# wq's first heads in one wide transfer at both ends of a decode kernel, w4 with two rows in a run, w3's weights with a step of two

## The chip, the cores and the metric

The kernel runs on one core of a Trainium2 chip. The metric is the device time of one execution in microseconds, as the median of several runs; smaller is better. The engines are named as in the profile: PE multiplies matrices (PEld is its loading of weights), DVE works on vectors, ACT computes activations, POOL is the general engine, and SP issues most transfers. Sixteen DMA engines carry the transfers.

## The reference

Two layers of attention with a cache and a small mixer with an MLP, for 8 rows of one token each:

```python
def _A_ref(x, k_cache, v_cache, wq, wo):      # x: 8 x 1 x 448
    q = (x @ wq) -> 16 heads of 256           # 8 K/V heads, each for 2 q heads
    scores = q . k * 256 ** -0.5              # 4096 cached keys
    o = softmax(scores) @ v
    return o @ wo
def _B_ref(x, w1, w2, w3, w4):
    x1 = x + shifted(gelu(norm(x) @ w1)) @ w2 # one token: every shift leaves zeros
    return x1 + gelu(norm(x1) @ w3) @ w4      # w3: 448 x 1792, w4: 1792 x 448
x = x + _A_ref(norm(x), ...); x = x + _B_ref(norm(x), ...)     # twice, same weights and cache
```

With one token the shifted part is zero, so the mixer comes down to the MLP on a norm of a norm. All inputs are bf16. The K and V caches hold 128 MiB each and are read in both layers, but for what stays in SBUF between them.

## The kernel before, in words

**Units and items.** The 8 K/V heads are taken in four pairs, gp 0 to 3. A unit is (ps, b, gp): layer ps (0 or 1), row b, pair gp. A unit has four K tiles and four V tiles of 1 MiB each (128 x 4096 bf16). `block` writes the order of the work out by hand, as a list of items: (unit, 0, c) is K tile c, (unit, 1, c) is V tile c, and (task, 2, 0) is a set of weights. Units of gp 2 and 3 of one row come in layer 0 and right behind it in layer 1, and some of their tiles (`kept`, `inner`, `part`) stay in SBUF or PSUM in between, so that they are read once.

**What an item does.** A K tile is turned by DVE in blocks (L1000), then PE computes scores (L1015), tiles 0 and 1 together and 2 and 3 together; ACT takes the exponential (L1024). A V tile is multiplied with the probabilities (L1083; in the last row's units with V as the weights, two columns apart, L1099). When a row has all its heads, a chain of small steps follows: scaling, wo (L180, L453), norm, w3, gelu, w4, the next layer's q. After each row's units come stages in which only V tiles are left, with the chain's steps between.

**Places and the queue.** SBUF has NC = 17 places of 1 MiB (L61). `emit_loads` (L939) runs after each item: it takes the next load of the list and issues it on SP as soon as a place is free, strictly in order; when the first in line has no place, it stops. A K pair wants two neighbouring places and one transfer of 2 MiB (L918, `load_k`): `reserve` (L881) holds two neighbours for it, free now or free within SOON = 8 items, and the line waits for them. Where none can be held, the two tiles go as single transfers of 1 MiB. V tiles go at L932, or in two halves at L935 in the stages with the chain. Each transfer waits on SP until what read its place before is done.

**Weights.** q of the first eight heads (gp 0 and 1) is computed from wq's first 2048 columns, which don't stay in SBUF. They are loaded again when needed, 1024 columns (one gp) into one place: `weights("q", (gp, r0, r1))` makes an item for gp and rows r0 to r1, `load_weights` (L980) issues three runs of 128 rows in one transfer (L989) and the last 64 rows by `load_tail` (L976), and the item computes q with `tail_cols` and `project_rows` (L391, L371). This is done seven times: gp 0 and gp 1 at the start for all rows of layer 0 (L799), three times under way for layer 1 (`q_rows`, L706), and at the end for gp 1, rows 5 to 7, and gp 0, row 7 (`q_final`, L707, L812 and L816). wq's other half, wo's second half, w3 and w4 stay in SBUF and are loaded at the start (L1143 to L1150); w4 by

```python
    nc.sync.dma_start(w4_sb[:], B_w4.rearrange("(c p) d -> p c d", p=128))
```

so that partition p holds rows p, 128 + p and so on, each a run of 448 elements (896 B). Block c of the hidden layer (128 of 1792) is computed from w3 by `wblk` (L214), which gives 128 neighbouring columns as weights, in `mlp_hidden` (L474) and in the last row's end (L1544); w4 is then read by block c (`w4_of`, and L1588 at the end).

**The end.** After the last V tile come its product, wo, the norm, w3 (L1544), gelu, w4 (L1588) and the transfer of the result (L1599).

Of the kernel before, what the change touches and what calls it, by code (L numbers as in the profile page):

```python
# [17 lines left out]
def kernel(  # L18
# [27 lines left out]
    nc = tc.nc  # L46
    Bn, Sq, D = A_x.shape
# [4 lines left out]
    Hq = HD // Dh  # L52
    F = B_w3.shape[1]
    assert Sq == 1 and Hq == 2 * G and Dh == 256 and S == 4096 and G % 2 == 0
    assert D == 448 and F % 256 == 0
    GP = G // 2
    NB2 = HD // 128
    HC = F // 128
# [163 lines left out]

    def rows_to_cols(row, nb):

# [236 lines left out]
    def mlp_hidden(b0, nb):  # L464

        yield from norm(xT[:, :, b0 : b0 + nb], nb, True)
        h_ps = room_ps("h", nb)
        for c in range(HC):
            for fc in range(4):
                w, xi = wblk(w3_sb, F, c, fc)  # L470
                if nb == 1:
                    wide(h_ps[:, c : c + 1], w, xbs(1)[:, xi, :], fc == 0, fc == 3)
                    continue
                nc.tensor.matmul(  # L474
                    h_ps[:, c * nb : c * nb + nb],
                    w,
                    xbs(nb)[:, xi, :],
                    start=(fc == 0),
                    stop=(fc == 3),
                )  # L480
            if c in (4, 9, HC - 1) if nb == 1 else c % 7 == 6:
                yield 0 if c == HC - 1 else None
        g_t = chn.tile([128, HC * MID], FP32, tag="g")
        hh = g_t[:, 0 : HC * nb]
        g0 = g_t[:, HC : 2 * HC] if nb == 1 else misc[:, 456 : 456 + HC * nb]
        if nb == 1:
            HT_t = chn.tile([128, HC, 1], BF16, tag="HT")
            HT = HT_t[:]
        else:
            HT = HTw[:, :, b0 : b0 + nb]  # L490

        nc.vector.tensor_scalar_mul(hh, h_ps, 0.5)
        nc.vector.scalar_tensor_tensor(g0, hh, 4 * 0.044715, hh, ALU.mult, ALU.mult)
        nc.vector.scalar_tensor_tensor(g0, g0, 1.0, hh, ALU.add, ALU.mult)
        nc.scalar.activation(g0, g0, ACT.Tanh, scale=2 * 0.7978845608028654)
        yield 0
        nc.vector.scalar_tensor_tensor(
            HT,
            g0.rearrange("p (c b) -> p c b", b=nb),
            1.0,  # L500
            hh.rearrange("p (c b) -> p c b", b=nb),
            ALU.add,
            ALU.mult,
        )
        yield 2
        return HT
# [197 lines left out]
    ]  # L704

    q_rows = {4: (0, 0, 4), 5: (1, 0, 5), 7: (0, 4, 7)}  # L706
    q_final = [(1, 5, 8), (0, 7, 8)]  # L707

    o_rows = {0: [(0, 4, 0, 3), (4, 8, 0, 1)], 3: [(0, 4, 3, 8), (4, 8, 3, 5)]}
    o_late = {1: (4, 8, 1, 2), 2: (4, 8, 2, 3), 5: (4, 8, 5, 8)}  # L710
# [42 lines left out]
    def weights(kind, rows):  # L753

        n = len(tasks)
        tasks.append((2, rows, kind))
        items.append((n, 2, 0))
# [37 lines left out]
        items.extend(due[:n])  # L795
        del due[:n]

    for gp in free:
        weights("q", (gp, 0, Bn))  # L799
    before = None  # L800
    for k in begin:
        block(k, before)
# [2 lines left out]
    for b in range(Bn):  # L805
        k3, k2 = ((1, b, gp) for gp in keep[::-1])
        block(k3)
        block(k2, k3)
        if b + 1 < Bn:
            first_kept(b + 1, ahead[b + 1], k2)  # L810
        else:
            weights("q", q_final[0])  # L812
            before = k2
            for k in final_units:
                if k == final_units[2]:
                    weights("q", q_final[1])  # L816
                block(k, before)
                if before == k2:
                    weights("o", None)
                before = k  # L820
            block(None, before)
# [117 lines left out]
    def emit_loads(most=None):  # L939
        n = 0  # L940
        while loads and places and n != most:
            it = loads[0]
            k, kv, c = it
            mate = (k, 0, c + 1)
            if kv == 0 and c % 2 == 0 and paired(k, c) and mate in loads[:4]:
                if it not in held:
                    reserve(it, mate)
                if it in held:
                    p = held[it]
                    if p in places and p + 1 in places:  # L950
                        del held[it], held[mate]
                        taken(it, p)
                        taken(mate, p + 1)
                        load_k(it, p, 2)
                        n += 1
                        continue
                    break
            open_ = open_places()
            if not open_:
                break  # L960
            p = pick(open_)
            taken(it, p)
            n += 1
            if kv == 2:
                load_weights(slots[p], tasks[k][2], tasks[k][1])
            elif kv:
                load_v(it, slots[p])
            else:
                both = c == 1 and (k, 0, 2) in loads[:2] and p + 1 in open_
                if both:  # L970
                    taken((k, 0, 2), p + 1)
                load_k(it, p, 1 + both)
# [7 lines left out]
    def load_weights(dst, kind, rows):  # L980

        if kind == "o":
            nc.sync.dma_start(
                dst[:, 0 : WI * D].rearrange("p (h x) -> p h x", x=2 * D),
                A_wo[0 : WI * 128].rearrange("(h p j) d -> p h (j d)", p=128, j=2),
            )
            return
        src = A_wq[:, HU * rows[0] : HU * rows[0] + HU]
        nc.sync.dma_start(  # L989
            dst[:, 0 : 3 * HU].rearrange("p (f c) -> p f c", f=3),  # L990
            src[0:384].rearrange("(f p) c -> p f c", f=3),
        )
        load_tail(dst[:, 3 * HU : 3 * HU + HU // 2], src)

    def transpose_k(t):

# [121 lines left out]
    nc.scalar.dma_start(x_row, A_x.rearrange("b s d -> (b s) d"))  # L1118
    tails = NC - 4
    places.remove(tails)  # L1120
    emit_loads(2)
    ps0 = rows_to_cols(x_row, Bn)
    nc.vector.tensor_copy(xT[:], ps0)
    emit_loads(5)
# [22 lines left out]
        A_wo[WI * 128 :].rearrange("(h p j) d -> p h (j d)", p=128, j=2),  # L1147
    )
    load_split(w3_sb, B_w3, F)
    nc.sync.dma_start(w4_sb[:], B_w4.rearrange("(c p) d -> p c d", p=128))  # L1150
    run(norm(xT[:], Bn, False))

    gens, pairs_done, p_of = [], {}, {}
# [104 lines left out]
        nc.scalar.copy(ptw[:, ring_of[it], :, 6:8], psv[slot_of[it[0]]][:, it[2]])  # L1258

    rz_gp = None  # L1260
    kept_q = items[12]

    for idx, it in enumerate(items):
        if idx == len(items) - 2:
# [24 lines left out]
        if kv == 2:  # L1289
            rows = b  # L1290
            if gp == "o" and rows is None:
                end_wo = slot
                early_rows(0, HH, 0, MID, 1, slot)
                add_gen("rest", rest(), idx + 1, idx + 18, 20)
            elif gp == "o":
                for who in rows:
                    early_rows(*who, 0, slot)
            else:
                gp_q, r0, r1 = rows
                nb = r1 - r0  # L1300

                def q_of_block(c, fc, qw=slot):
                    if fc < 3:
                        return qw[:, fc * HU + 128 * c : fc * HU + 128 * c + 128], fc
                    k = 2 * 128 * c // HU
                    at = 3 * HU + 128 * c - k * HU // 2
                    return qw[:, at : at + 128], 3 + k

                ps_q = (
                    store[0][:, 256 : 256 + 8 * nb] if nb == Bn else misc[:, 192 : 192 + 8 * nb]  # L1310
                )
                cols = tail_cols(r0, r1, misc[:, 320 : 320 + nb], slot[:, 4 * HU - 128 :])
                project_rows(q_of_block, 4 * gp_q, 4, r0, r1, ps_q, cols)
                if idx > 1:
                    q_rows_done.update((r, gp_q) for r in range(r0, r1))
        elif kv == 0:
            if (ps, b) not in state:
                if ps == 1:
# [133 lines left out]
                pairs_done[ps, b] = pairs_done.get((ps, b), 0) + 1  # L1452
                free_slots.append(slot_of.pop(n))
        if kv == 2:
            if gp == "q" or rows is not None:
                places.append(p)
        elif not (ps == 0 and stays(it)):
            if (ps, gp, kv, c) == (1, keep[1], 1, homes[0]):
                where[(b, part[0]), part[1:]] = p
                moves.extend(part_words(slot))  # L1460
            elif (ps, gp, kv, c) == (1, keep[1], 1, homes[1]):
                where[(b, inner[0]), inner[1:]] = p
                moves.extend(inner_words(slot))
            elif kv == 0 and kept_now:
                if c % 2 == 0:
                    places.extend([p, where[(b, gp), (0, c + 1)]])
            elif not late(it):
                places.append(p)
            elif c % 2:
                places.extend([where[n, 0, c - 1], p])  # L1470
# [69 lines left out]
    for f0, f1 in ((0, 3), (3, 4)):  # L1540
        for c in range(HC):
            for fc in range(f0, f1):
                w, xi = wblk(w3_sb, F, c, fc)
                nc.tensor.matmul(  # L1544
                    h_ps[:, c * nb : c * nb + nb],
                    w,
                    xe[:, xi, :],
                    start=(c + fc == 0),
                    stop=(fc == 3),
                    skip_group_check=True,  # L1550
                )
# [80 lines left out]
```

## Time and profile before

The runs took 1036.71 to 1040.44 us.

| what | value |
|---|---|
| median of 3 runs | 1037.01 us |
| profiled execution | 1035.63 us, its span 1033.6 us |
| PE matmul busy | 655.7 us (63%), 12739 instructions |
| DVE busy | 597.4 us (58%) |
| ACT busy | 211.6 us (20%) |
| HBM read | 419.63 MB, 406 GB/s over the span |
| wq loads of 768 KB and of 128 KB | 7 and 7, 12.9 and 12.4 us from issue to landing |
| w4's load (1568 KB) | 1, 15.1 us from issue to landing |
| K loads of 2048 KB and of 1024 KB | 86 and 20 |
| granted TensorE clock, mean | 0.631 |

The profile is that of one execution. Busy shares are averages over stages with different limits; the slices (40 equal parts of the span, a digit or a rate for each) show how they follow each other. A row of a group gives the line, the engine, the operation, its shapes and count, the busy time and the mean of one in ns, and then the idle time just before and what ended it. A row of the timeline gives the start and the time taken in us and how many instructions were merged; for SP, the time of a merged row spans the waits inside it. A row of a window gives the busy time and count of PE, PEld, DVE, ACT and POOL, the granted clock, the DMA engines' share and GB/s. The trace also holds a record of every DMA packet, with its start, its length and its bytes.

### The profile page before, as it was taken

How to read it: one execution, taken by the hardware profiler on the slowest of the kernel's cores; microseconds unless marked ns; L12 is line 12 of the kernel's file. 1: busy time of each engine (PE TensorE's matmuls, PEld its weight loads, DVE VectorE, ACT ScalarE, POOL GpSimd, SP SyncE). 2: the span in 40 equal slices, each digit the busy share in tenths (PEclk: the TensorE clock that was granted, in tenths of full speed). 3: DMA queues.
4: the chain of work that ended last, by engine and by line, in shares of the span. 5: the costliest groups of instructions: out<-in, count | busy, mean ns of one | idle time of the engine just before them, and what ended most of it. 6: DMA issues, size and time to landing. Idle time of an engine off the chain costs nothing.

```text
span 1033.6 us, 28857 instructions
## 1 busy us (share of the span) xinstructions
PE 655.7 (63%) x12739; PEld 417.7 (40%) x12739; DVE 597.4 (58%) x1407; ACT 211.6 (20%) x685; POOL 16.4 (2%) x27
## 2 busy tenths in 40 slices
PE   3144544875577567755785578557756875586775
PEld 2022222553345334533453346334533553355544
DVE  6334567148825871597249725792597259725572
ACT  0011111131214120412041214121412141214110
POOL 0000000000000000000000000000000000000000
PEclk9976555566666556655566665556665575656655
DMA  9999999999999999999999999999999999999994
GB/s 364 390 426 420 423 423 419 390 424 424 416 402 422 424 417 401 419 425 398 407 412 425 418 399 412 423 418 399 426 424 416 401 414 425 418 401 411 418 422 199
DMA packets 68141, 421.51 MB, mean 408 GB/s; under 512 B 6952, under 2 KB 12848, under 8 KB 43312
## 3 DMA queue, kind: packets, MB, share of 16 engines
q1 hardware_dynamic: 67968, 419.66, 99.1%
q8 instruction: 100, 1.64, 0.6%
q14 instruction: 25, 0.20, 0.0%
q10 hardware_dynamic: 48, 0.01, 0.0%
HBM read 419.63 MB, written 0.01 MB: 406 GB/s over the span
## 4 chain that ended last, share of the span: by engine, by line
DMA 43%; DVE 27%; PE 22%; issue 3%; SPq 3%; ACT 2%; POOL 0%; DVEq 0%; ACTq 0%
DMA places<-in_A_v_cache_dram 28%; DVE places L1000 22%; DMA places<-in_A_k_cache_dram 14%; PE sc L1015 9%; PE o L1083 6%; PE misc L592 2%; PE misc L180 2%; ACT p_n L1024 2%; DVE qbd L415 1%; DVE store L1046 1%; DMA places<-in_A_wq_dram 1%; PE misc L529 1%; SPq L932 1%; SPq L199 1%; PE misc L1066 1%
## 5 line engine op out<-in xcount | busy, mean ns | idle before, releaser
L1000 DVE STREAM_TRANSPOSE places<-places 128x512 uint32<-128x512 uint32 (+1 forms) x576 | 455.1, 853 | 39.8 <-DMA places<-in_A_k_cache_dram 39.3
L1015 PE MATMUL sc<-places,qbd 128*8 128x256 bf16 (+1 forms) x4768 | 236.3, 352 | 164.8 <-DVE places L1000 163.9
L1083 PE MATMUL o<-places,ptw 128*8 128x256 bf16 x3808 | 242.9, 380 | 129.4 <-DMA places<-in_A_v_cache_dram 100.6
L1015 PEld LDWEIGHTS <-qbd 128*8 128x8 bf16 x4768 | 124.2, 105 | 231.6 <-DVE places L1000 123.5
L1083 PEld LDWEIGHTS <-ptw 128*8 128x8 bf16 x3968 | 102.4, 101 | 192.7 <-issue 116.6
L1024 ACT ACTIVATE p_n<-sc 128x256 bf16<-128x256 f32 x128 | 95.5, 746 | 351.0 <-PE sc L1015 346.8
L1258 ACT COPY ptw<-psv 128x32 bf16<-128x32 bf16 x248 | 52.8, 227 | 175.4 <-PE o L1083 173.8
L415 DVE CAST qbd<-misc 32x16 bf16<-32x16 f32 (+1 forms) x184 | 30.8, 168 | 62.0 <-PE misc L409 60.2
L592 PE MATMUL misc<-R_t,o_t 128*128 128x4 f32 (+1 forms) x212 | 45.5, 321 | 29.1 <-DVE qbd L415 12.4
L592 PEld LDWEIGHTS misc<-R_t,o_t 128*128 128x128 f32 x212 | 41.2, 271 | 45.4 <-issue 16.6
L532 DVE RECIPROCAL rz<-misc 128x4 f32<-128x4 f32 (+1 forms) x55 | 9.6, 175 | 83.1 <-PE misc L529 45.7
L1073 ACT CAST psv<-misc 128x128 bf16<-128x128 f32 x64 | 17.0, 266 | 188.1 <-PE misc L1066 188.1
L1051 ACT COPY places<-store 128x1024 bf16<-128x1024 bf16 x40 | 40.2, 1027 | 11.0 <-PE o L1083 11.0
L529 PE MATMUL misc<-zm,one 128*128 128x4 f32 (+1 forms) x110 | 28.0, 326 | 17.0 <-DVE zm L521 13.0
L529 PEld LDWEIGHTS misc<-zm,one 128*128 128x128 f32 x110 | 23.2, 263 | 32.8 <-DVE zm L521 16.0
L180 PEld LDWEIGHTS <-w_sb 128*128 128x128 bf16 x896 | 27.7, 105 | 16.7 <-issue 16.7
L1024 ACT ACTIVATION_READ_ACCUMULATOR p_n<-sc 128x1 f32 x128 | 33.9, 265 | 0.0
L546 ACT COPY o_t<-o 128x256 f32<-128x256 f32 x53 | 19.8, 373 | 47.0 <-PE o L1083 47.0
L295 POOL TENSOR_TENSOR t<-t,nhalf 128x2 f32<-128x2 f32 (+2 forms) x18 | 12.0, 671 | 951.4 <-DVE t L316 951.4
L1046 DVE TENSOR_SCALAR store<-places 128x512 uint32<-128x512 uint32 x40 | 25.0, 678 | 0.0
L1066 PEld LDWEIGHTS <-p_n 128*128 128x128 bf16 x256 | 11.5, 105 | 30.0 <-issue 18.9
L596 DVE CAST qT<-misc 128x8 bf16<-128x8 f32 (+1 forms) x37 | 7.2, 195 | 27.0 <-PE misc L592 20.3
(158 smaller groups left out, 368.8 us busy)
## 6 DMA issues: line engine op xcount, KB each, us to landing
places<-in_A_k_cache_dram SPq DMA_DIRECT2D x86, 2048.0 KB, 14.3
places<-in_A_v_cache_dram SPq DMA_DIRECT2D x194, 512.0 KB, 7.2
places<-in_A_v_cache_dram SPq DMA_DIRECT2D x87, 1024.0 KB, 18.2
places<-in_A_k_cache_dram SPq DMA_DIRECT2D x20, 1024.0 KB, 11.8
places<-in_A_wq_dram SPq DMA_DIRECT2D x7, 768.0 KB, 12.9
rest<-in_A_v_cache_dram SPq DMA_DIRECT2D x8, 640.0 KB, 14.2
places<-in_A_v_cache_dram SPq DMA_DIRECT2D x8, 384.0 KB, 13.1
wo_sb<-in_A_wo_dram SPq DMA_DIRECT2D x1, 2688.0 KB
```

Of the source, the lines that this page charges most:

```text
L180: nc.tensor.matmul(bass.AP(out.tensor, out.offset, [out.ap[0], (1, WIDE)]), w, x.to_broadcast([128, WIDE]), start=start, stop=stop, skip_g ...
L415: nc.vector.tensor_copy(qbd[32 * a : 32 * a + 32, :, g0 : g0 + ng, a, :], qs.rearrange("p e (f g u h) -> p (e f) u g h", f=2, u=2, h=2)[:, ...
L529: nc.tensor.matmul(z_ps, ones, zm[:], start=True, stop=True)
L592: nc.tensor.matmul(ot_ps[:, j], o_sb[:].rearrange("p (i j) -> p j i", j=2)[:, j], R, start=True, stop=True)
L1000: nc.vector.transpose(w, w)
L1015: nc.tensor.matmul(sc[32 * k : 32 * k + 8, 128 * (x % 2) : 128 * (x % 2 + nx)], qbd[:, ep, gp % 2].rearrange("p a h -> p (a h)"), v, start ...
L1024: nc.scalar.activation(p_sb[:, :, :, 2 * u : 2 * u + 2].rearrange("p t i x -> p x t i"), sc[:, 0:256].rearrange("p (x t i) -> p x t i", x= ...
L1046: nc.vector.tensor_single_scalar(kept_words.bitcast(U32), words.bitcast(U32), 0, op=ALU.bitwise_or)
L1051: nc.scalar.copy(words, kept_words.bitcast(BF16))
L1066: nc.tensor.matmul(pt_ps[:, t], p_sb[:, t].rearrange("p i x -> p (i x)"), cols, start=True, stop=True,)
L1083: nc.tensor.matmul(o_ps[32 * q : 32 * q + 8, :], ptz[:, at : at + 8], v[:, y * Dh : (y + 1) * Dh] if v2 is None or y < PR else v2[:, (y - ...
L1258: nc.scalar.copy(ptw[:, ring_of[it], :, 6:8], psv[slot_of[it[0]]][:, it[2]])
```

## The change

Three edits, and what they carry with them:

- At the start and at the end the two wq loads become one of a new kind, "q2": 2048 columns into two neighbouring places, one item, one `tail_cols` for the rows of both, and then both projections. The last row's gp 0 is thereby computed with gp 1's rows, ahead of the final units, and not before the third of them. The list of items is one shorter from the start on, and two at the end.
- `emit_loads` gives a "q2" load the place p only where p + 1 is open too, and else stops.
- w4 is loaded so that two of its rows lie in one run (1792 B) for 12 of 14 blocks, in three transfers; w3's blocks take every second of 256 columns to fit that order (`w3blk`), and two of the 14 blocks stay as they were.

```diff
+    def w3blk(c, fc):
+
+        at = fc * F + 128 * c if fc < 3 else 3 * F + 128 * (c % 7)
+        xi = fc if fc < 3 else 4 - c // 7
+        if c % 7 == 6:
+            return w3_sb[:, at : at + 128], xi
+        at -= 127 * (c % 7 % 2)
+        return w3_sb[:, at : at + 255 : 2], xi
...
-                w, xi = wblk(w3_sb, F, c, fc)
+                w, xi = w3blk(c, fc)
...
-    q_final = [(1, 5, 8), (0, 7, 8)]
+    q_first = ((0, 0, Bn), (1, 0, Bn))
+    q_final = ((1, 5, 8), (0, 7, 8))
...
-    for gp in free:
-        weights("q", (gp, 0, Bn))
+    weights("q2", q_first)
...
-            weights("q", q_final[0])
+            weights("q2", q_final)
             before = k2
             for k in final_units:
-                if k == final_units[2]:
-                    weights("q", q_final[1])
                 block(k, before)
...
+            wide_q = kv == 2 and tasks[k][2] == "q2"
+            if wide_q:
+                open_ = [p for p in open_ if p + 1 in open_]
+                if not open_:
+                    break
             p = pick(open_)
             taken(it, p)
             n += 1
+            if wide_q:
+                places.remove(p + 1)
+                free_at[p + 1] = free_at[p]
...
-        src = A_wq[:, HU * rows[0] : HU * rows[0] + HU]
+        at, n = (0, HF) if kind == "q2" else (HU * rows[0], HU)
+        src = A_wq[:, at : at + n]
         nc.sync.dma_start(
-            dst[:, 0 : 3 * HU].rearrange("p (f c) -> p f c", f=3),
+            dst[:, 0 : 3 * n].rearrange("p (f c) -> p f c", f=3),
             src[0:384].rearrange("(f p) c -> p f c", f=3),
         )
-        load_tail(dst[:, 3 * HU : 3 * HU + HU // 2], src)
+        load_tail(dst[:, 3 * n : 3 * n + n // 2], src)
...
-    emit_loads(2)
+    emit_loads(1)
...
-    nc.sync.dma_start(w4_sb[:], B_w4.rearrange("(c p) d -> p c d", p=128))
+    w4_rows = B_w4.rearrange("(k x) d -> k x d", k=2)
+    w4_to = w4_sb[:].rearrange("p (k c) d -> p k c d", k=2)
+    for k in range(2):
+        nc.sync.dma_start(
+            w4_to[:, k, 0:6].rearrange("p (c j) d -> p c (j d)", j=2),
+            w4_rows[k, 0:768].rearrange("(c p j) d -> p c (j d)", p=128, j=2),
+        )
+    nc.sync.dma_start(w4_to[:, :, 6], w4_rows[:, 768:].rearrange("k p d -> p k d"))
```

The projection loop of the item takes its columns from both places where the kind is "q2" (768 rows of runs of 2048 B become 384 runs of 4096 B; the last 64 rows come in runs of 2048 B where they came in runs of 1024 B).

More of the change, by code (lines that the diff above doesn't have):

```diff
@@ L54 @@
     assert Sq == 1 and Hq == 2 * G and Dh == 256 and S == 4096 and G % 2 == 0
-    assert D == 448 and F % 256 == 0
+    assert D == 448 and F == 14 * 128
     GP = G // 2
@@ L963, in emit_loads @@
             n += 1
+            if wide_q:
+                places.remove(p + 1)
+                free_at[p + 1] = free_at[p]
             if kv == 2:
-                load_weights(slots[p], tasks[k][2], tasks[k][1])
+                load_weights(places_t[:, p * PB : (p + 1 + wide_q) * PB], tasks[k][2], tasks[k][1])
             elif kv:
@@ L1260 @@
     rz_gp = None
-    kept_q = items[12]
+    kept_q = items[11]
     for idx, it in enumerate(items):
@@ L1298, with q_of_block @@
             else:
[L1299 to L1310, printed above, removed]
-                )
[L1312 to L1315, printed above, removed]
+                n_gp = 2 if gp == "q2" else 1
+                parts = rows if n_gp == 2 else [rows]
+                n_w = n_gp * HU
+                qw = places_t[:, p * PB : (p + n_gp) * PB]
+                r_at, r_to = parts[0][1:]
+                cols = tail_cols(
+                    r_at, r_to, misc[:, 320 : 320 + r_to - r_at], qw[:, n_gp * PB - 128 :]
+                )
+                for gp_q, r0, r1 in parts:
+                    nb = r1 - r0
+                    def q_of_block(c, fc, c0=(n_gp - 1) * 8 * gp_q):
+                        at = 128 * (c0 + c)
+                        if fc < 3:
+                            return qw[:, fc * n_w + at : fc * n_w + at + 128], fc
+                        k = 2 * at // n_w
+                        at += 3 * n_w - k * n_w // 2
+                        return qw[:, at : at + 128], 3 + k
+                    ps_q = (
+                        store[gp_q][:, 256 : 256 + 8 * nb]
+                        if nb == Bn
+                        else misc[:, 192 : 192 + 8 * nb]
+                    )
+                    project_rows(
+                        q_of_block,
+                        4 * gp_q,
+                        4,
+                        r0,
+                        r1,
+                        ps_q,
+                        lambda xi: cols(xi)[:, r0 - r_at : r1 - r_at],
+                    )
+                    if idx > 0:
+                        q_rows_done.update((r, gp_q) for r in range(r0, r1))
         elif kv == 0:
@@ L1454 @@
         if kv == 2:
-            if gp == "q" or rows is not None:
-                places.append(p)
+            if rows is not None:
+                places.extend([p, p + 1] if gp == "q2" else [p])
         elif not (ps == 0 and stays(it)):
@@ L1542 @@
             for fc in range(f0, f1):
-                w, xi = wblk(w3_sb, F, c, fc)
+                w, xi = w3blk(c, fc)
                 nc.tensor.matmul(
```

## Prediction

> **What bounds the kernel now.** I read the page's slices first, then the waits by group, then the DMA queue's own list in the stretches that the change touches, then the tail.
>
> ```profile
> span 1033.6 us, 28857 instructions
> ...
> DMA  9999999999999999999999999999999999999994
> GB/s 364 390 426 420 423 423 419 390 424 424 416 402 422 424 417 401 419 425 398 407 412 425 418 399 412 423 418 399 426 424 416 401 414 425 418 401 411 418 422 199
> ...
> L1083 PE MATMUL o<-places,ptw 128*8 128x256 bf16 x3808 | 242.9, 380 | 129.4 <-DMA places<-in_A_v_cache_dram 100.6
> ```
>
> The DMA row is 9 in every slice but the last: the 16 engines move 419.6 MB without a pause. PE's PV matmuls idle 129.4 us, 100.6 of them for V. In the trace's packet records the engines are full from about 7 us to 1022 us. So the time is the start, plus packet time over 16, plus a tail of some 11.6 us after the last V piece (1022.0 to 1033.6). Two things move it: shorter packet time, or a moment in which the engines run dry, which nothing gives back later because they never rest later.
>
> The profiled execution is 1035.63 us (span 1033.6 and 2.0 around it); the median of the runs is 1037.01, 1.4 more. I sum differences and add them to the median.
>
> **Packets (removed work).** Mean time of one packet, from the packet records of the whole trace: 896 B 46.5 ns, 1024 B 46.2, 1792 B 78.2, 2048 B 91.2, 4096 B 165.2, 8192 B 315.3, 16384 B 623.8.
> - w4 lands early (45.1 to 52.4 us); its 1792 packets of 896 B took 46.0 ns there, 1792 B ones (wo, just ahead) 79.1. Now 1792 x 46.0 = 82.4 us; after 768 x 79.1 + 256 x 46.0 = 72.5 us. Over 16 engines: -0.62 us.
> - Each pair of wq loads has 768 packets of 2048 B and 256 of 1024 B (81.9 us); after, 384 of 4096 B and 128 of 2048 B (75.1 us): -0.42 us. Two pairs: -0.84. At the start 2048 B packets took 101.6 ns, elsewhere 85.6 between wq packets alone, so the first pair may give 0.23 to 0.95.
> - Start: the second wq load is late to reach the engines:
>
> ```profile
> 4.50:6.50 2.00, 0.61 (x2) 0.50 (x2) 0.78 (x6) 0.00 (x0) 0.43 (x1) 1.00 0.73 212
> ```
>
> DMA share 0.73 over 2 us is 0.54 us lost. With two issues fewer (about 1.4 us of SP) K stands ready sooner: 0 to -0.54, I take -0.3.
>
> The Trainium skill, "DMA: Bandwidth & Descriptors", Specifications, gives 512 B as the smallest transfer at line rate; by it all these packets would run at one rate. The rows disagree (896 B in 46.5 ns is 19 B/ns, 8192 B in 315.3 is 26), so I keep the rows, and that rule stands below as a rival.
>
> **Two neighbouring places (added wait).** The wide load needs places p and p+1 open, and emit_loads stops when the first in line can't go: what stands behind it on SP waits too. It also shifts which place every later load gets. Both programs as built load in the same order; 306 tiles get another place. For each load, the item after which it can go is set against the trace: when PE ends that item, and when the bytes ahead of the load have landed. The second less the first is the queue's lead. Now it is 1.6 us at the least, with full engines; in the changed program it is less than that in two spots alone.
>
> *Spot 1, K of (pass 1, b 1, gp 0), around 550 us.* Now its tiles 0 and 1 go as two single loads after (1,3,2)'s scores, 2 and 3 as one after a V item:
>
> ```profile
> 526.27 15.38 SPq L918 DMA_DIRECT2D places<-in_A_k_cache_dram  x5
> 541.70 0.43 SPq L932 DMA_DIRECT2D places<-in_A_v_cache_dram  x1
> 550.58 0.33 SPq L918 DMA_DIRECT2D places<-in_A_k_cache_dram  x1
> ```
>
> In the changed program tiles 0 and 1 go together after the V item that ends at 538.7, and tiles 2 and 3 are tied to places 0 and 1, which hold K tiles 0 and 1 of (1,0,0). Those are read by the scores that end at 550.5, and the V load behind waits with them:
>
> ```profile
> 544.40 2.43 DVE L1000 STREAM_TRANSPOSE places<-places 128x1024 uint32<-128x1024 uint32 x3
> 547.05 5.86 DVE L1000 STREAM_TRANSPOSE places<-places 128x1024 uint32<-128x1024 uint32 x7
> 549.51 1.02 PE L1015 MATMUL sc<-places,qbd 128*8 128x256 bf16 x16
> ```
>
> Those scores can't come sooner: DVE turns their K from 544.4 on, behind the q projection and the K ahead of it, at 2.4 us a tile, all data landed. All that was issued before tiles 2 and 3 has landed at 547.0 (bytes summed over the packets). So the engines are dry from 547.0 to the first packets of a load issued at 550.58. How long from issue to packet on idle engines: the wq load issued at 929.95 has its first at 931.52, 1.57 us; the first load of the program 1.1 us, with all 16 engines busy after some 2.0. I take 1.6: 550.58 + 1.6 - 547.0 = **+5.2 us**. Bounds: 4.7 to 5.6 by the two rows, and 0 if the scores came early enough. (The same page, Latency and other measured facts, has 0.6 us to the first byte; by it the sum would be 1.0 us less. The row says 1.57.) The K in question then lands near 557, and DVE needs it near 560, so compute doesn't notice; the next V stage, which waits for V, then runs 5 us late.
>
> *Spot 2, the last wide load, near 930 us.*
>
> ```profile
> 925.12 2.81 SPq L935 DMA_DIRECT2D places<-in_A_v_cache_dram  x3
> 929.95 0.38 SPq L989 DMA_DIRECT2D places<-in_A_wq_dram  x1
> 930.38 0.55 SPq L976 DMA_DIRECT2D places<-in_A_wq_dram  x1
> 931.87 2.34 SPq L918 DMA_DIRECT2D places<-in_A_k_cache_dram  x3
> ```
>
> At 929.95 one place comes free (a V), which serves wq now. A pair comes free only with the kept K's scores, which release the next line at 931.87. So wq goes 1.9 us later, its first packets near 933.4. The V still outstanding at 930.0 is 239 packets of 4096 B: 239 / 16 x 165 ns = 2.5 us, to 932.5 on the mean engine. That is 1.0 us dry, of which 0.2 is there now (14.8 busy engines around 931): **+0.8**, bounds 0 and 1.9. Behind it SP has K at once.
>
> **At nothing.** (a) The second final projection moves some 20 items earlier: 32 weight loads and matmuls at L371 (0.9 us) and a few DVE rows, one tail_cols less; its two DMAs pass K of (1,5,1) and (1,6,1), wo and a V, which land 2.2 us later and have 8 us and more of lead. The end waits for V that was issued 17 us ahead, and hides it; without that cover it costs about 1 us. (b) At the start both projections wait for all of wq, near 7 us, but the norm ends at 8.3 anyway. (c) w3's weights with a step of two elements: 48 of each 56. The trace has such a load already, L1099 (V's every second column), beside the plain ones:
>
> ```profile
> L1099 PEld LDWEIGHTS <-places 128*128 128x128 bf16 x256 | 7.5, 104 | 6.6 <-DMA places<-in_A_v_cache_dram 6.2 <-issue 0.4
> L1544 PEld LDWEIGHTS <-w_sb 128*128 128x128 bf16 x56 | 1.8, 107 | 0.6 <-issue 0.6
> ```
>
> 104 against 107 ns: nothing.
>
> **Sum.** -0.62 - 0.84 - 0.3 + 5.2 + 0.8 = +4.2 us: 1039.9 for the profiled execution, **1041.3** on the median, +0.41%. A measurement of this kernel tells about 0.5% (5.2 us) from no change, so this counts as the same, on the slow side.
>
> **Rivals.**
> - *Not slower: the bytes alone.* If DVE reaches (1,0,0) some 5 us sooner against the queue, spot 1 closes. For it: the lead in items there (9) is more than the smallest now (6). Against: DVE is busy without a gap from 531 to 540 and from 544.4 on. Then -1.76 + 0.8, or -1.76 with spot 2 covered too: 1035.3 to 1036.1. Chance 0.18.
> - *Slower by over 0.5%: spot 1 is longer.* The engines refill late after running dry, as at the start, where the second load takes until 6.5 us to fill all 16 although issued by 2.8. Of that delay, 1 to 2 us more would fall on the same gap; it decides when the gap passes 6.2 us. 1042.3 to 1043.3. Chance 0.14.
> - *Strided weights cost.* If each of the 48 in the final w3 pass stood alone on the path at 105 ns: +5.0 in the tail, 1046.3. Against: L1099. Chance 0.04.
> - *Packets of 896 B and up all run at one rate* (the rule above): the 1.46 us of packets aren't saved: 1042.7. Against: the packet rows. Chance 0.04.
>
> My forecast has 0.60, with its own range of 1040 to 1042.5 (its top passes +5.2 with about 0.05). Faster by over 0.5% would need 5.2 us less, three times all packets saved: 0.01. Slower by over 0.5%: 0.05 + 0.14 + 0.04 + 0.04 = 0.27. Within: 0.72. The range that holds 8 in 10: 1036.0 to 1044.0, which takes in the bytes alone and the longer gap.
>
> **What would show it.** Right: in the changed profile SP issues one 2 MB K load and a V right after scores, near 550, after a pause of some 12 us; the GB/s drops there by about 5 us' worth in one slice, the V waits of the stage after lie 5 us later; packets of 896 B fall from some 1800 to 264 and w4 lands in 0.6 us less; wq's last load comes from L1005 right after scores near 932; L1544's successor keeps 105 ns. Wrong: full DMA through 550 (then the first rival), a w3 pass longer than 1.7 us, or an end that no longer waits for V.

## The result and the profile after

The changed kernel takes 1040.38 us (median of 16 runs, 1037.75 to 1042.96) against 1037.02 us for the kernel before on the same chips (16 runs): a ratio of 1.0029, 95% interval 1.0018 to 1.0040, so 1.9 to 4.1 us slower. Forecast was +4.2 us and 1041.3 us. The profiled execution of the changed kernel took 1042.26 us, 1.9 above its median; where times are compared, the medians and ratios are meant, and the profile is used to see where the time lies.

The page of the changed kernel, its slices first, then the group of the PV matmuls (the lines have moved by some 16; L1083 is now L1099, L1015 is L1031, L1000 is L1016; the L1099 that the prediction shows, V's every second column, is L1115 now):

```profile
span 1040.2 us, 28728 instructions
...
DMA  9999999999999999999998999999999999999994
GB/s 377 394 428 421 420 424 419 401 423 422 416 403 425 426 412 397 419 406 407 390 415 335 420 408 416 425 418 378 425 425 417 403 418 423 417 394 404 422 421 194
...
L1099 PE MATMUL o<-places,ptw 128*8 128x256 bf16 x3808 | 246.0, 383 | 133.9 <-DMA places<-in_A_v_cache_dram 105.4
```

One slice stands out: number 22 (546 to 572 us) has 335 GB/s where it had 425, and its DMA digit is the one 8 among the 9s. PE's wait for V grew from 100.6 to 105.4 us. The next view is SP's own list around that slice in the changed kernel (start, time, engine, line, transfer, count; the first row is a merged one and spans its waits):

```profile
526.23 12.61 SPq L925 DMA_DIRECT2D places<-in_A_k_cache_dram  x3
```

```profile
550.70 0.33 SPq L925 DMA_DIRECT2D places<-in_A_k_cache_dram  x1
551.08 0.42 SPq L939 DMA_DIRECT2D places<-in_A_v_cache_dram  x1
```

After a K load near 538.8 SP issues nothing until 550.70. Before, it issued another K load near 541.3 and a V load at 541.70. What released it at 550.70 are PE's scores, which themselves wait for DVE. The two rows of PE in the changed kernel, with the idle time before and its releaser in brackets, and DVE's:

```profile
548.45 1.03 PE L1031 MATMUL sc<-places,qbd 128*8 128x256 bf16 x16 [4.70 <-DVE places L1016]
...
549.63 1.02 PE L1031 MATMUL sc<-places,qbd 128*8 128x256 bf16 x16
```

```profile
544.52 2.43 DVE L1016 STREAM_TRANSPOSE places<-places 128x1024 uint32<-128x1024 uint32 x3
...
547.16 7.05 DVE L1016 STREAM_TRANSPOSE places<-places 128x1024 uint32<-128x1024 uint32 x9
```

The scores end at 550.65 and the load goes 0.05 us later. The window of 545 to 555 us (columns as before: busy time of PE, PEld, DVE, ACT, POOL, granted clock, DMA share, GB/s), in the kernel before:

```profile
545.00:555.00 10.00, 5.18 (x96) 3.23 (x100) 9.89 (x19) 1.16 (x5) 0.00 (x0) 0.50 1.02 428
```

and in the changed one:

```profile
545.00:555.00 10.00, 5.07 (x96) 3.15 (x100) 9.89 (x19) 1.05 (x4) 0.00 (x0) 0.50 0.53 197
```

PE, PEld and DVE have the same number of instructions in it, and DVE is busy for 9.89 of 10 us in both. The DMA share falls by 0.49 over 10 us, which is 4.9 us of all 16 engines. From the packet records, the mean engine is dry (has no packet in flight) for 4.7 us between 540 and 556. The last load ahead of the gap ends with one small record of 4 B on each engine: these 16 end from 546.35 to 548.75, at 547.05 on the mean. The first new packet starts at 551.67, the sixteenth at 552.27, and the mean of these 16 is 551.86.

The start of the kernel after, 4.5 to 6.5 us, shows the small gain there (DMA share 0.73 before; 0.22 more over 2 us is 0.4 us):

```profile
4.50:6.50 2.00, 0.61 (x2) 0.50 (x2) 0.77 (x5) 0.00 (x0) 0.44 (x1) 1.00 0.95 346
```

### The profile page after: what moved, and what is told of

Same layout as the page of the kernel before. It is cut to its first block, busy times and chain, and to the rows that moved or that the text cites. A ratio compares the mean times of both kernels' runs of the same rounds, so it can differ in the third digit from the quotient of the medians.

```text
span 1040.2 us, 28728 instructions
## 1 busy us (share of the span) xinstructions
PE 663.0 (64%) x12673; PEld 420.1 (40%) x12673; DVE 597.3 (57%) x1403; ACT 211.6 (20%) x685; POOL 16.4 (2%) x27
## 4 chain that ended last, share of the span: by engine, by line
DMA 42%; DVE 28%; PE 22%; ACT 2%; issue 2%; SPq 2%; POOL 0%; DVEq 0%; ACTq 0%
DMA places<-in_A_v_cache_dram 27%; DVE places L1016 23%; DMA places<-in_A_k_cache_dram 14%; PE sc L1031 9%; PE o L1099 6%; PE misc L601 2%; PE misc L180 2%; DVE store L1062 2%; ACT p_n L1040 2%; DVE qbd L424 1%; PE misc L538 1%; DMA places<-in_A_wo_dram 1%; SPq L199 1%; PE misc L1082 1%; PE misc L380 0%
## 5 line engine op out<-in xcount | busy, mean ns | idle before, releaser
L1016 DVE STREAM_TRANSPOSE places<-places 128x512 uint32<-128x512 uint32 (+1 forms) x576 | 455.4, 854 | 46.7 <-DMA places<-in_A_k_cache_dram 46.5
L1031 PE MATMUL sc<-places,qbd 128*8 128x256 bf16 (+1 forms) x4704 | 238.9, 357 | 163.3 <-DVE places L1016 162.1
L1099 PE MATMUL o<-places,ptw 128*8 128x256 bf16 x3808 | 246.0, 383 | 133.9 <-DMA places<-in_A_v_cache_dram 105.4
L1031 PEld LDWEIGHTS <-qbd 128*8 128x8 bf16 x4704 | 123.3, 105 | 232.3 <-DVE places L1016 124.8
L1099 PEld LDWEIGHTS <-ptw 128*8 128x8 bf16 x3968 | 102.8, 101 | 198.1 <-issue 121.6
L601 PE MATMUL misc<-R_t,o_t 128*128 128x4 f32 (+1 forms) x212 | 47.6, 331 | 32.2 <-DVE qbd L424 16.9
L601 PEld LDWEIGHTS misc<-R_t,o_t 128*128 128x128 f32 x212 | 43.3, 284 | 49.4 <-issue 22.0
```

The lines of the kernel that those rows point to most:

```text
L601: nc.tensor.matmul(ot_ps[:, j], o_sb[:].rearrange("p (i j) -> p j i", j=2)[:, j], R, start=True, stop=True)
L1016: nc.vector.transpose(w, w)
L1031: nc.tensor.matmul(sc[32 * k : 32 * k + 8, 128 * (x % 2) : 128 * (x % 2 + nx)], qbd[:, ep, gp % 2].rearrange("p a h -> p (a h)"), v, start ...
L1099: nc.tensor.matmul(o_ps[32 * q : 32 * q + 8, :], ptz[:, at : at + 8], v[:, y * Dh : (y + 1) * Dh] if v2 is None or y < PR else v2[:, (y - ...
```

## The experiments

The theory on record: the wide loads shift the places of all loads behind them; one K pair then has to wait for a pair of places that is read late, the DMA engines run dry, and that time is lost. Its main rival: the wait is hidden by what lies in SBUF, and the time comes from w3's weights with a step of two, or from the moved projection. All kernels below were timed in turn with the kernel before, in two sets: 29 runs of it in each (medians 1037.50 and 1037.61 us), 12 of each variant, and 6 of place8. The dry times come from the one execution of each that was profiled.

**old_places: the places alone, without the change.**

```diff
 # the kernel before, emit_loads
-            p = pick(open_)
+            p = (10, 11)[n] if kv == 2 and now[0] == 0 else pick(open_)
```

> The kernel before with one thing altered: the two first wq loads go to places 10 and 11 in place of 0 and 1. Nothing of the change is in it. The plan of places then ties K tiles 2 and 3 of (1,1,0) to a pair that is read by the scores of (1,0,0), as in the changed kernel. Theory 1 (the time comes from the place wait near 550 us): SP issues that K load some 9 us later than before, the DMA engines are dry for 4.5 to 5 us there, and the time is 4.5 us above the kernel before (ratio 1.0045). Theory 2 (the wait is hidden by what is stored ahead, and the changed kernel's extra time comes from the w3 weights with a step of two or from the projection that was moved): no difference, ratio 1.000.

Measured: 1041.08 us, ratio 1.0033 (1.0018 to 1.0049). Nothing was computed or loaded otherwise than before, and the time of the changed kernel came back. SP's list in this kernel:

```profile
550.62 0.33 SPq L918 DMA_DIRECT2D places<-in_A_k_cache_dram  x1
551.00 0.43 SPq L932 DMA_DIRECT2D places<-in_A_v_cache_dram  x1
```

and its window:

```profile
545.00:555.00 10.00, 5.14 (x96) 3.17 (x100) 9.89 (x19) 1.12 (x5) 0.00 (x0) 0.50 0.51 186
```

The engines are dry for 5.0 us. Theory 2 can't explain this time: there is no w3 step and no moved projection here. The ratio of 1.0045 that was expected lies inside the interval, near its top.

**place10: the whole change, with other places.**

```diff
 # the changed kernel, emit_loads
-            p = pick(open_)
+            p = 10 if wide_q and now[0] == 0 else pick(open_)
```

> The changed kernel, with its first wide wq load put at places 10 and 11 in place of 0 and 1; by the plan no K pair then waits near 550 us. Theory 1: the dry stretch is gone, the time is 4.7 us below the changed kernel and 1.2 to 1.7 us below the kernel before (ratio 0.9985). Theory 2: it stays where the changed kernel is, ratio 1.003.

Measured: 1036.40 us, ratio 0.9992 (0.9980 to 1.0005). Its interval lies below that of the changed kernel. No dry time from 540 to 556:

```profile
545.00:555.00 10.00, 5.13 (x96) 3.17 (x100) 9.89 (x19) 1.11 (x5) 0.00 (x0) 0.50 1.00 423
```

By this kernel's plan tiles 2 and 3 of (1,1,0) get places 3 and 4, which come free with the q item; they go at 542.5 with the V behind them, and the load released by the scores at 550.6 is already the next K pair, (1,2,0):

```profile
524.14 18.73 SPq L925 DMA_DIRECT2D places<-in_A_k_cache_dram  x4
542.97 0.38 SPq L939 DMA_DIRECT2D places<-in_A_v_cache_dram  x1
550.62 0.33 SPq L925 DMA_DIRECT2D places<-in_A_k_cache_dram  x1
```

The gain over the kernel before (0.8 us by the ratio) is less than the 1.2 to 1.7 expected and not told from none.

**place8: a second wait of the kind.** The same line with 8 in place of 10.

> The changed kernel with its first wide wq load at places 8 and 9. By the plan the K pair near 550 us waits as in the changed kernel, and a second one, tiles 2 and 3 of (1,5,0) near 870 us, waits too, with a lead of -2.4 us. Theory 1: two dry stretches, 4.7 and about 4 us, so 4 us above the changed kernel, ratio to before 1.007. Theory 2: as the changed kernel, 1.003.

Measured: 1044.54 us, ratio 1.0067 (1.0044 to 1.0090), 3.9 us above the changed kernel by the ratios. Both stretches of this kernel are dry, the second for 5.2 us (4 expected):

```profile
545.00:555.00 10.00, 5.55 (x104) 3.35 (x104) 9.89 (x19) 1.52 (x5) 0.00 (x0) 0.50 0.51 185
860.00:870.00 10.00, 4.99 (x104) 2.93 (x104) 9.89 (x18) 1.83 (x7) 0.00 (x0) 0.71 0.49 179
```

The second lies where the plan of places said. Twice the wait makes about twice the time, by 6 runs.

**w4_alone: w4 and w3 without the wide loads.**

```diff
 # the kernel before, with the change's w3blk and its three w4 transfers
-                w, xi = wblk(w3_sb, F, c, fc)
+                w, xi = w3blk(c, fc)
...
-    nc.sync.dma_start(w4_sb[:], B_w4.rearrange("(c p) d -> p c d", p=128))
+    for k in range(2):
+        nc.sync.dma_start(
+            w4_to[:, k, 0:6].rearrange("p (c j) d -> p c (j d)", j=2),
+            w4_rows[k, 0:768].rearrange("(c p j) d -> p c (j d)", p=128, j=2),
+        )
+    nc.sync.dma_start(w4_to[:, :, 6], w4_rows[:, 768:].rearrange("k p d -> p k d"))
```

> The kernel before with the w4 and w3 edit alone; places as before. Theory 1: w4 lands with 0.6 to 0.7 us less packet time, the w3 pass at the end is as long as before (1.5 to 1.6 us for 56 weight loads), ratio 0.9993. Theory 2 (the step of two costs): the w3 pass is longer and the time 1 to 5 us above the kernel before, ratio 1.001 to 1.005.

Measured: 1036.79 us, ratio 0.9988 (0.9976 to 1.0000). The two w3 passes with the step (first the one for rows 0 to 3, then the one at the end) have the same mean as with plain weights. The first row below is of the kernel before, where L474 is what is now L483 (the end's plain row, L1544, stands in the prediction); the others are of this kernel:

```profile
L474 PEld LDWEIGHTS <-w_sb 128*128 128x128 bf16 x56 | 1.9, 107 | 0.1
```

```profile
L483 PEld LDWEIGHTS <-w_sb 128*128 128x128 bf16 x56 | 1.8, 107 | 0.0
L1560 PEld LDWEIGHTS <-w_sb 128*128 128x128 bf16 x56 | 1.8, 107 | 0.6 <-issue 0.6
```

So the step of two costs nothing that shows (107 ns in all three rows), and no sign of the 1 to 5 us of theory 2 is left.

**first_wide and last_wide: one wide load each.**

```diff
 # first_wide: the changed kernel, the end as before
-            weights("q2", q_final)
+            weights("q", q_final[0])
             before = k2
             for k in final_units:
+                if k == final_units[2]:
+                    weights("q", q_final[1])
 # last_wide: the changed kernel, the start as before
-    weights("q2", q_first)
+    for part_q in q_first:
+        weights("q", part_q)
...
```

> The changed kernel with its last wide wq load taken back to two single ones; the first wide load, w4 and w3 stay changed. By the plan the K pair near 550 us waits as in the changed kernel. Theory 1: the dry stretch of 4.5 to 5 us is there, ratio to before 1.003 to 1.004; so it is the first wide load that brings it, by moving the places of all that follows. Rival (the dry stretch comes from the two-place rule itself, at the load that needs the pair): no dry stretch near 550, ratio 0.999.

> The changed kernel with its first wide wq load taken back to two single ones; the last wide load, w4 and w3 stay changed. Theory 1: no dry stretch near 550 us; the wide load near 930 us goes some 1.9 us later than before, which costs 0.2 to 0.8 us of dry engines, against 0.7 us saved by w4; ratio 0.999 to 1.000. Rival (as with first_wide): the time is that of the changed kernel, ratio 1.003.

Measured: first_wide 1040.32 us, ratio 1.0023 (1.0007 to 1.0040), dry for 5.1 us near 550; last_wide 1038.11 us, ratio 0.9995 (0.9984 to 1.0006), no dry time there. The same window, first_wide's row and then last_wide's:

```profile
545.00:555.00 10.00, 4.50 (x96) 2.71 (x100) 9.93 (x17) 1.06 (x4) 0.00 (x0) 0.66 0.49 180
```

```profile
545.00:555.00 10.00, 3.73 (x63) 2.30 (x62) 9.18 (x18) 1.06 (x4) 0.00 (x0) 0.66 1.01 424
```

It is the first wide load, 540 us ahead of the loss, that brings it, and old_places and place10 show that it does so through the places alone: the loss comes without any wide load, and goes with the wide load kept. That the order in which its two places are given back (both after one item, where they came back after one item each) sets the later choices is read from the source, not tried by itself. The rule of two open places itself, at the last load, costs little:

```profile
933.09 0.38 SPq L1006 DMA_DIRECT2D places<-in_A_wq_dram  x1
933.52 0.66 SPq L992 DMA_DIRECT2D places<-in_A_wq_dram  x1
934.27 2.26 SPq L926 DMA_DIRECT2D places<-in_A_k_cache_dram  x3
```

In last_wide, wq and K now go on one release, as forecast, and the engines are dry there for 0.06 us more than in the kernel before.

**soon6: a rule that doesn't wait so long.**

```diff
 # the changed kernel
-    SOON = 8
+    SOON = 6
```

> The changed kernel with one number altered: a K pair waits for two neighbours only where both come free within 6 items, not 8. Near 550 us its tiles then go as single loads as they did before the change. Theory 1: no dry stretch, ratio to before 0.999, whatever place the first load has; 23 in place of 19 pairs lie apart, which lengthens their scores on PE a little. Rival (the wait is needed, and single loads cost as much in packets and in PE time): ratio 1.002 or more.

Measured: 1037.22 us, ratio 0.9990 (0.9977 to 1.0002), no dry time from 540 to 556, although nothing was put at a chosen place:

```profile
523.71 16.76 SPq L925 DMA_DIRECT2D places<-in_A_k_cache_dram  x5
540.52 0.42 SPq L939 DMA_DIRECT2D places<-in_A_v_cache_dram  x1
547.97 0.33 SPq L925 DMA_DIRECT2D places<-in_A_k_cache_dram  x1
```

By this kernel's plan tiles 0 and 1 of (1,1,0) went as single loads, near 528 us, and tiles 2 and 3 as a pair to places that the q item left; the load at 547.97 is (1,2,0)'s. Of all versions, place10, soon6 and w4_alone stand lowest, clearly below the changed kernel. They are 0.1% below the kernel before: place10 and soon6 are not told from it, and w4_alone's interval ends at 1.0000.

## Why the prediction was right, step by step

The forecast of a small loss held, and for the reason given. Its terms, each against what was measured (dry times from single profiled executions):

| step | forecast, us | measured, us |
|---|---|---|
| spot 1, K pair near 550 | +5.2 (4.7 to 5.6) | +4.7 dry (old_places 5.0, first_wide 5.1) |
| spot 2, last wide load | +0.8 (0 to 1.9) | +0.2 dry, over the 0.1 of before (0.06 to 0.97 in the other kernels that have it) |
| w4's packets | -0.62 | -0.73 |
| wq's packets, both pairs | -0.84 | -0.14 at the start, +0.1 to +0.2 at the end |
| start | -0.3 | -0.4 (DMA share 0.73 to 0.95 over 2 us) |
| sum | +4.2 | +3.8 by these; timed +3.0 (1.9 to 4.1) |

The total came nearer than its terms, which is luck in part: the two spots were priced 1.1 us too high together, and the 0.84 us of wq's packets, which were not saved, made up for most of that.

- **Spot 1** was right in mechanism and place: which load waits, for which scores, and that DVE holds these back. The price of the restart was not. The prediction read 1.57 us from issue to packet on idle engines off the wq load at 929.95, but those engines weren't idle: the packet records of the kernel before have all 16 at work until 931.4. After the gap the first packet came 0.97 us after the issue (550.70 to 551.67), the sixteenth 1.57, and the mean of the 16 is 1.16. That the sixteenth repeats the 1.57 is chance. The dry time of the mean engine goes by the mean: the engines ended at 547.05 (547.0 forecast), the load went 0.12 us later than forecast, and 1.16 in place of 1.6 makes the gap 4.8 us by these figures, 4.7 by the time with no packet in flight. The Trainium skill's first-byte latency of 0.6 us ("DMA: Bandwidth & Descriptors", Latency and other measured facts) is below all three; the trace's figures are taken here.
- **Compute didn't notice**, as forecast: PE and DVE do the same in the window, and PE's V waits grow instead. That most of the loss isn't given back is shown by old_places and place8.
- **Spot 2** was too high in the changed kernel. Why was not traced. The other kernels with the last wide load show 0.06, 0.34, 0.73 and 0.97 us more than the kernel before, so 0.8 is inside what occurs.
- **wq's packets** were mis-sized, the one term with nothing left of it. The prediction took 165.2 ns for a 4096 B packet from V halves. wq's at the start took 200.1 ns (384 packets), its last 64 rows 84.0: 384 x 200.1 + 128 x 84.0 = 87.6 us against 768 x 101.6 + 256 x 46.0 = 89.8, so 0.14 us over 16 engines. At the end wq's packets can't be told from V halves of the same size. All 4096 B packets of the last 2 us ahead of the last rows had a mean of 193 ns, the last 384 of them 188. By 193 it is 384 x 193 + 128 x 84 = 84.9 us against 81.7 before, 0.2 us more over 16 engines; by 188 it is 0.1.
- **w4**: 1792 packets of 896 B took 5.16 us over 16 engines; now 256 of 896 B take 0.69 and 768 more of 1792 B 3.74. So the same bytes took 14% less packet time in longer runs. The smallest transfer at line rate that the Trainium skill gives, 512 B ("DMA: Bandwidth & Descriptors", Specifications), would make the two equal; the prediction had it as a rival, and these figures speak against it.
- **The rivals**: the bytes alone is near what place10, soon6 and last_wide show when the wait is taken away (ratios 0.9990 to 0.9995, none told from 1); a longer gap didn't come (all engines run 1.57 us after the issue); strided weights cost nothing (107 ns).

Left open: the time grows by less than the dry time. old_places is dry for 5.0 us and 3.4 us slower (1.9 to 5.1); place8 is dry for 10.1 us and 6.9 us slower (4.6 to 9.3), with about 1 us of packets and start to its credit. The intervals reach from all of it down to less than half (old_places) or about half (place8). Small dry moments elsewhere don't explain it: outside the spots named here, between 12 and 1015 us, the profile of the kernel before has 1.1 us of them and those of all the others 1.3 to 2.4 (the changed kernel 2.4, some of it at 460 to 470 and 705 to 715 us, where the forecast named no spot), which should add time and not save it. Each of these profiles is one execution, and the one of the kernel before was 1.4 us below its median, that of the changed kernel 1.9 above. So how much of a dry microsecond the time keeps isn't settled.

## What to carry to other kernels

Where one queue issues in strict order into a fixed set of places, an edit to any load moves the places of all that follow: compare the whole plan, load by load, with the time at which the bytes ahead of each will have landed, not only the load that was edited. A place that is freed late costs nothing until a load stands in line for exactly that place with nothing left in flight; a shorter limit on the wait for neighbours, or another place for the first load, took the whole loss away. The cost of a packet is to be taken from the same tensor and the same stage: the same 4096 B took 165 ns from V over the whole run and 200 from wq at the start. And the time from issue to packet is to be read off engines that are idle when the load is issued.

## What the runs showed of the hardware that was not expected

A run of 4096 B of wq, cut from rows of 8192 B, took 200 ns a packet at the start and, with V halves among them, 188 to 193 near the end of the changed kernel, where V's halves of 4096 B (also cut from runs of 8192 B) took 165 to 166; two packets of 2048 B of wq took 203 ns at the start. Doubling the run of this tensor therefore bought next to nothing here, while doubling most of w4's runs from 896 B to 1792 B bought 14%. Why wq's packets are slow was not tried.
